# Two cached-attention layers, one core: the order of PE's and ACT's work at the change of layers

## The chip, the cores and the metric

The kernel runs on one core of a Trainium2 chip. The metric is the device time of one execution in microseconds, the median of several runs; lower is better. The profile is that of one further execution. Its engines are PE (matmuls; the loading of a stationary operand is shown apart, as PEld), DVE, ACT and POOL, and SP, which here only issues transfers. The kernel's name for the 128-partition on-chip memory that holds all large data is `mem`; `tps`, `sps` and `mps` are buffers in the accumulator memory that PE writes to (PSUM).

## The reference

Two layers are computed for a batch of 2 and one new token each (D = 576). Each layer is attention over a cache and then a mixer with an MLP, each behind a layer norm and added to x:

```python
# attention: H = 32 heads, Sk = 16384 cached positions, Dh = 128
q = (x @ wq).reshape(B, Sq, H, Dh).transpose(0, 2, 1, 3)
scores = jnp.einsum("bhqd,bhkd->bhqk", q, k_cache) * (Dh ** -0.5)
p = _softmax(scores, axis=-1)
o = jnp.einsum("bhqk,bhkd->bhqd", p, v_cache)
return o.transpose(0, 2, 1, 3).reshape(B, Sq, H * Dh) @ wo
# mixer and MLP: F = 4608
h = _gelu(_layernorm(x) @ w1)            # its columns are then shifted along S, which is 1
x1 = x + hs @ w2                         # hs: the shifted columns
return x1 + _gelu(_layernorm(x1) @ w3) @ w4

x = x + _A_ref(_layernorm(x), K, V, wq, wo)
x = x + _B_ref(_layernorm(x), w1, w2, w3, w4)     # and both once more, with the same weights and cache
```

With S = 1 the shifted columns are zero, so the mixer adds nothing; the kernel still multiplies zeros by w2. K and V are 268 MB each in bfloat16 and are read in both layers; the weights are some 20 MB per layer.

## The kernel before, in words

**Units.** There are 64 units (2 batches x 32 heads), numbered u. The K of a unit is a tile of 4 MB, 128 partitions x 128 blocks of 128 values, its V another. `mem` has six slots of one tile each and ahead of them a small region (AUX, `kt`) that holds three transposed chunks; a chunk is 8 blocks. In the main loop (`attention`, L994 to L1056, a hardware loop over three units a turn) half of the blocks of a K tile are transposed on PE (`transposed`, L1148, matmuls at L1158, into one of four buffers `tps`), copied to `kt` by ACT (`evacuate`, L1174) and multiplied by q on PE (`scores`, L1184); the other half are multiplied and summed by DVE (`dots`, L1215 and L1219), with q broadcast to all partitions (`q_broadcast`, L1112: DVE makes `diag`, L1115, PE multiplies, L1119, ACT copies, L1122). One unit behind follow the softmax (`softmax_max`: DVE, then POOL for the maximum over partitions, L1232; `softmax_exp`: ACT, L1240 to L1246) and the product with V (`pv`, L1272, four groups of 32 matmuls; a step of `keep_o` copies the result away).

**Order of the work.** Every engine executes its own list in order. `Graph` records each operation when the Python code calls it, so the order of calls is the order on each engine, and derives the semaphore waits from the named buffers that an operation reads and writes. An operation recorded with `to=` signals one engine alone; if another engine has to wait for it, it waits for the next operation of the same engine without `to=` (`_stand_in`). All transfers are issued by SP in the order of a plan (`plan_all`); `Store.pump` issues the next one as soon as its place in `mem` is free, in the order of the queue and never past one that has to wait.

**The change of layers.** Layer 1 takes the units in the order 63, 61, 62, 0, 1, ... and finds K of units 61 to 63 and V of 62 and 63 still in five of the slots. Slot 0 (with AUX) is all that is free for the weights: wo of layer 0, w3, w4, wq of layer 1, and then V of unit 61 in four parts. Each of these pieces lies where earlier ones lay, so it can be issued when PE has multiplied those. K of unit 0 then goes to the slot of K63, K of unit 1 in two halves to that of K61, V0, K2, V1 and so on to the next.

Between the loops run, in this order: `last_head` (the last scores, softmax and PV of layer 0, and wo: `shares` and `normed` divide by the sums, `dealt` lays the heads' outputs out for wo as `oA`, three quarters of the heads, and `oB`, the last quarter; `heads_projection`, matmuls at L893, multiplies wo's five pieces), `two_norms`, `cols_projection` with w3 (L823, L833; six pieces), `gelu_z`, `groups_projection` with w4 (L893 again; eight pieces; `side_norm` among them), `input_norm` of layer 1, and `q_projection` with wq (L823, L833; five pieces).

Through all of this K63 is prepared for the first unit of layer 1. `ahead` (L668) has PE transpose a chunk of K63 into `tps`; `lay` (L686, ACT at L692) copies it back over its own place. 14 of its 16 chunks are done so. When q of layer 1 is known, `early_scores` (L1200) multiplies these chunks straight from their place by q: first the chunks of which DVE does the scores in other units (b of 32 and more in both halves), then the rest; the last two chunks of the second half are transposed only then and go the usual way. DVE copies the part of the scores that it would have made itself to `s_dve` (L1033) and enters the loop.

Where the calls of `ahead` and `lay` stand in the kernel before: in `last_head` of layer 0 ahead(2) behind `normed`, ahead(2) and lay(2) behind `dealt`, lay(2) behind `touch(ACT.Sqrt)`, ahead(1) behind the first piece of wo, ahead(2) and lay(2) behind the second and the third, lay(4) behind the last; in `two_norms` ahead(2) and lay(4); in w3 ahead(3) and lay(2) ahead of the last piece; behind each w4 piece but the first ahead(1) and lay(1), in `input_norm` ahead(2) and behind each wq piece but the last ahead(1) and lay(1), by which time little or nothing is left for them.

The first two pieces of wo need `oA` alone. In the kernel before all four groups of PV run first, then piece 0, the layout of `oB`, and pieces 1 to 4.

## Time and profile before

| what | before |
|---|---|
| median of 3 runs | 2562.14 us (2562.13 to 2563.07) |
| profiled execution | 2561.02 us |
| its span, from first to last instruction | 2559.2 us |
| PE, PEld busy | 64%, 62% |
| DVE, ACT busy | 74%, 47% |
| DMA: queue of the transfers | 99.7% of 16 engines' span, 1094.23 MB |
| read from HBM, over the span | 428 GB/s |

A line of a timeline gives the start in us from the span's start, the length in us, engine, line of the kernel, operation, what is written and read, the number of instructions merged, and in brackets the idle time of the engine before it with what ended it; "issue" means that nothing the profile shows was waited for. A line of a table by stretches gives the stretch and its length, busy time (and number of instructions) of PE, PEld, DVE, ACT and POOL, the granted clock of PE as a share of full speed, the DMA share and GB/s. SPq rows are transfers at their issue. A row of the transfers' list ends with size in KB and the us from issue to landing.

### The profile page before, as it was taken

The page shows a single profiled execution, that of the slowest core. Times are in us where ns is not written, and L with a number is a line of the kernel's source. Part 1 is how long each engine was busy: PE and PEld are TensorE (multiplying, and loading weights), DVE is VectorE, ACT ScalarE, POOL GpSimd, SP SyncE. Part 2 cuts the span into 40 slices and gives each one's busy share as a digit, 9 for nine tenths or more (in the row PEclk, how much of TensorE's full clock was granted, in tenths as well). Part 3 has the DMA queues.
Part 4 walks back from the last instruction along what each step waited for, and adds up shares of the span by engine and source line. Part 5 has one row for each costly group of instructions (what it writes and reads, how often), then busy time and mean ns, then how long its engine had stood idle before and what let it go on. Part 6 is the DMA issues. An engine that isn't in the chain of part 4 may idle for free.

```text
span 2559.2 us, 75096 instructions
## 1 busy us (share of the span) xinstructions
PE 1629.4 (64%) x34456; PEld 1593.6 (62%) x34456; DVE 1889.5 (74%) x1925; ACT 1214.9 (47%) x1831; POOL 162.2 (6%) x151
## 2 busy tenths in 40 slices
PE   3766666666656666665777756666665666666566
PEld 3666566656656666665767756665665665666566
DVE  5877777777777777777549877777777777777774
ACT  2544444544444454444445544454444444445442
POOL 0000000000000000000000000000000000000000
PEclk8655555555555565556555655555555556555555
DMA  9999999999999999999999999999999999999999
GB/s 410 428 432 433 431 431 433 431 431 432 433 430 432 433 430 433 432 431 431 411 374 428 433 431 431 433 431 430 433 433 431 431 433 431 431 433 432 430 434 379
DMA packets 44762, 1094.82 MB, mean 428 GB/s; under 512 B 4907, under 2 KB 6319, under 8 KB 9391
## 3 DMA queue, kind: packets, MB, share of 16 engines
q1 hardware_dynamic: 44718, 1094.23, 99.7%
q8 instruction: 29, 0.48, 0.1%
q14 instruction: 15, 0.11, 0.0%
HBM read 1094.21 MB, written 0.00 MB: 428 GB/s over the span
## 4 chain that ended last, share of the span: by engine, by line
DMA 66%; DVE 19%; issue 8%; PE 6%; DVEq 0%; ACT 0%; SPq 0%; POOLq 0%; ACTq 0%
DMA mem<-in_A_k_cache_dram 64%; DVE prod L1215 9%; DVE s_dve L1219 8%; PE tps L1158 2%; DMA mem<-in_B_w_dram 2%; PE mps L1272 2%; PE sps L1119 1%; DMA mem<-in_A_wq_dram 0%; PE sps L1184 0%; PE sps L893 0%; DVE diag L1115 0%; DVE mx L1229 0%; PE sps L823 0%; DVE q_col L1109 0%; DVE o_acc L1253 0%
## 5 line engine op out<-in xcount | busy, mean ns | idle before, releaser
L1174 ACT ACTIVATE mem<-tps 128x1024 bf16<-128x1024 bf16 x1018 | 1029.4, 1023 | 848.9 <-PE tps L1158 827.0
L1219 DVE TENSOR_REDUCE s_dve<-prod 128x16 f32<-128x2048 bf16 x508 | 1161.2, 2286 | 17.4
L1158 PE MATMUL tps<-ident,mem 128*128 128x128 bf16 x8256 | 1010.9, 301 | 151.0 <-POOLq L187 147.7
L1215 DVE TENSOR_TENSOR prod<-mem,qb 128x2048 bf16<-128x2048 bf16 x508 | 621.4, 1223 | 537.0 <-POOLq L187 516.0
L1272 PE MATMUL mps<-p,mem 128*128 128x1 bf16 x16384 | 515.0, 166 | 608.1 <-ACT p L1246 608.1
L1272 PEld LDWEIGHTS mps<-p,mem 128*128 128x128 bf16 x16384 | 487.5, 104 | 618.8 <-ACT p L1246 618.8
L1158 PEld LDWEIGHTS tps<-ident,mem 128*128 128x128 bf16 x8256 | 770.8, 136 | 160.8 <-POOLq L187 157.0
L1184 PEld LDWEIGHTS sps<-q_col,mem 128*128 128x128 bf16 x8144 | 410.8, 114 | 4.7 <-ACT mem L1174 4.7
L1184 PE MATMUL sps<-q_col,mem 128*128 128x1 bf16 x8144 | 398.3, 170 | 4.1 <-ACT mem L1174 3.9
L1232 POOL PARTITION_ALL_REDUCE mx<-mx x128 | 160.2, 1252 | 2344.2 <-DVE mx L1229 2344.2
L1240 ACT ACTIVATE mx<-mx 128x1 f32<-128x1 f32 x128 | 25.9, 203 | 340.0 <-POOL mx L1232 339.9
L1119 PE MATMUL sps<-diag,ones_bf 128*128 128x128 bf16 x129 | 37.1, 287 | 114.3 <-DVE diag L1115 114.3
L1119 PEld LDWEIGHTS sps<-diag,ones_bf 128*128 128x128 bf16 x129 | 13.5, 105 | 124.8 <-DVE diag L1115 124.8
L1122 ACT ACTIVATE qb<-sps 128x128 bf16<-128x128 f32 x129 | 35.7, 277 | 65.9 <-PE sps L1119 65.9
L1242 ACT ACTIVATE p<-s_dve,mx 128x64 bf16<-128x64 f32 x128 | 44.5, 348 | 15.5
L1246 ACT ACTIVATE p<-sps,mx 128x64 bf16<-128x64 f32 x128 | 37.5, 293 | 0.0
L1227 DVE TENSOR_REDUCE mx<-sps 128x1 f32<-128x64 f32 x128 | 27.4, 214 | 7.3 <-PE sps L1184 7.3
L1115 DVE TENSOR_SCALAR diag<-ident,q_f 128x128 bf16<-128x128 bf16 x129 | 31.5, 244 | 0.0
L823 PE MATMUL sps<-xn,mem 128*128 128x2 bf16 x544 | 21.4, 174 | 9.4 <-DMA mem<-in_A_wq_dram 8.3
L823 PEld LDWEIGHTS sps<-xn,mem 128*128 128x128 bf16 x544 | 20.5, 122 | 10.1 <-DMA mem<-in_A_wq_dram 8.8
L1225 DVE TENSOR_REDUCE mx<-s_dve 128x1 f32<-128x64 f32 x128 | 26.7, 208 | 0.0
L1246 ACT ACTIVATION_READ_ACCUMULATOR p<-sps,mx (+1 forms) x128 | 24.2, 189 | 0.0
(112 smaller groups left out, 223.4 us busy)
## 6 DMA issues: line engine op xcount, KB each, us to landing
mem<-in_A_v_cache_dram SPq DMA_DIRECT2D x125, 4096.0 KB, 47.2
mem<-in_A_k_cache_dram SPq DMA_DIRECT2D x124, 4096.0 KB, 40.9
mem<-in_B_w_dram SPq DMA_DIRECT2D x10, 864.0 KB, 14.7
mem<-in_A_wq_dram SPq DMA_DIRECT2D x8, 1024.0 KB, 12.8
mem<-in_B_w_dram SPq DMA_DIRECT2D x7, 1152.0 KB, 15.7
mem<-in_A_wo_dram SPq DMA_DIRECT2D x6, 1152.0 KB, 35.8
mem<-in_A_v_cache_dram SPq DMA_DIRECT2D x4, 1024.0 KB, 8.8
mem<-in_A_k_cache_dram SPq DMA_DIRECT2D x2, 2048.0 KB, 13.1
```

Of the source, the lines that this page charges most:

```text
L823: ins = pe.matmul(out[:, m * B:(m + 1) * B], lhsT=buf[:, c:c + 127 * d + 1:d], rhs=self.xn[:, k, :], start=first and m == lo, stop=False, ...
L1119: self.pe(lambda pe: pe.matmul(qps, lhsT=self.ones_bf[:, :], rhs=self.diag[:, :], start=True, stop=True, skip_group_check=True), reads=["o ...
L1122: self.act(lambda e: e.activation(out=self.qb[s % self.NS][:, :], in_=qps, func=ACT.Copy), reads=[("qps", i)], writes=[("qb", s % self.NS) ...
L1158: ins = pe.transpose(self.tps[t][:, j * 128:(j + 1) * 128], buf[:, j * 128:(j + 1) * 128], self.ident[:, :])
L1174: self.act(lambda e: e.activation(out=self.kt[k], in_=self.tps[t][:, :].rearrange("p (i c) -> p i c", i=self.CH), func=ACT.Copy), reads=[( ...
L1184: ins = pe.matmul(self.sps[sp][:, c * self.CH + j:c * self.CH + j + 1], lhsT=self.kt[k][:, j, :], rhs=self.q_col[:, sp:sp + 1], start=True ...
L1215: self.dv(lambda e: e.tensor_tensor(out=prod, in0=buf.rearrange("p (j d) -> p j d", d=128), in1=qbc, op=ALU.mult), reads=[("qb", s % self. ...
L1219: self.dv(lambda e: e.tensor_reduce(out=sd[:, c0:c0 + DB], in_=prod, axis=AX.X, op=ALU.add), reads=["prod"], writes=[("s_dve", s % self.NS ...
L1232: self.pool(lambda e: e.partition_all_reduce(self.mx[:, 3, m:m + 1], self.mx[:, 2, m:m + 1], channels=128, reduce_op=ROP.max), reads=[("mx ...
L1242: self.act(lambda e: e.activation(out=p[:, n:self.NB], in_=self.s_dve[s % self.NS][:, :], func=ACT.Exp, bias=self.mx[:, 4, m:m + 1], scale ...
L1246: self.act(lambda e: e.activation(out=p[:, 0:n], in_=self.sps[i][:, 0:n], func=ACT.Exp, bias=self.mx[:, 4, m:m + 1], scale=self.scale, acc ...
L1272: ins = pe.matmul(self.mps[:, 448:449], lhsT=buf[:, j * 128:(j + 1) * 128], rhs=p[:, col:col + 1], start=(h == 0 and b == 0), stop=(h == 1 ...
```

## The change

Four things move; no operation of the reference's computation is added or left out.

- In `last_head`, piece 0 of wo is multiplied behind the first of the four groups of PV, and piece 1 behind the last, ahead of the layout of `oB`. All calls of `ahead` there go; one chunk is transposed at the end of `attention`, ahead of the last scores, and one `lay` stays, behind the softmax. The copy that makes `every` (the spread mask, L1068) stands ahead of `softmax_max`.
- The other chunks are transposed in `two_norms` (three), behind w3 (one), behind the first five pieces of w4 (one each), in `input_norm` (two, with their copies) and behind the first four pieces of wq (one each). The last two of these four are the two chunks that the kernel before transposed after q was known; they are kept in `tps` (`held_over`) until the loop's buffers are free.
- In `q_projection` of layer 1 the first unit's column of q is written straight to `q_col`, ahead of the copies to `q_f`.
- `early_scores` takes the chunks half by half, in the order of the blocks, and the broadcast for the next unit stands behind the second chunk instead of ahead of the first.

```diff
@@ __init__
+        self.held_over = []
@@ ahead
             if self.made == len(self.early):
-                return
+                if len(self.held_over) < self.LEAD:
+                    c = 2 * self.PB // self.CH - self.LEAD + len(self.held_over)
+                    self.transposes(1, 0, self.order(1)[0], c)
+                    self.held_over.append((0, self.order(1)[0], c, self.chunk))
+                    self.chunk += 1
+                continue
@@ input_norm
         self.touch(ACT.Exp)
+        self.lay(1 - l, 2)
@@ two_norms
-        self.ahead(l, 2)
+        self.ahead(l, 3)
@@ cols_projection
-            if w == "w3" and i == len(order) - 2:
-                self.ahead(l, 3)
-                self.lay(l, 2)
...
+        if w == "w3":
+            self.ahead(l, 1)
@@ q_projection
-        for s, u, n in self.runs(l):
+        if l:
+            at = self.order(l)[0]
+            self.dv(lambda e: e.tensor_copy(out=self.q_col[:, 0:1], in_=q[:, at:at + 1]),
+                    reads=[("sps", 2)], writes=[("q_col", 0)])
+        for s, u, n in self.runs(l)[l:]:
@@ groups_projection
-            if i >= 1:
+            if i < 5:
                 self.ahead(l, 1)
+            if i < 6:
                 self.lay(l, 1)
@@ attention
-            self.q_column(0)
-            self.q_broadcast(1)
-            for h, b, col in self.early:
+            pend += self.held_over
+            for h, b, col in sorted(self.early):
                 self.early_scores(l, o[0], h * self.BP + b, col)
-            for c in range(2 * n - LEAD, 2 * n):
-                self.transposes(l, 0, o[0], c)
-                pend.append((0, o[0], c, self.chunk))
-                self.chunk += 1
+                if (h, b) == (0, self.CH):
+                    self.q_broadcast(1)
...
         self.g.loop(first, (U - 1) // NS, NS)
+        self.ahead(l, 1)
         while pend:
@@ last_head
+        self.dv(... self.every ...)
         self.softmax_max(s)
         self.keep_o(s - 1)
-        self.dv(... self.every ...)
         self.shares(0, first)
         self.normed(l, 0, first)
-        self.ahead(l, 2)
         self.dealt(0, late, self.sps[2], ("sps", 2), self.masked[0], self.oA[:, :], "oA")
-        self.ahead(l, 2)
-        self.lay(l, 2)
         self.softmax_exp(s)
         self.touch(ACT.Sqrt)
-        self.lay(l, 2)
+        self.lay(l, 1)
         self.shares(first, U)
         self.landed("v", u, False)
-        for g in range(4):
+        self.pv(l, s, u, 0)
+        self.heads_projection(l, 0)
+        for g in range(1, 4):
             self.pv(l, s, u, g)
         self.keep_o(s, None)
         self.normed(l, first, U)
-        self.heads_projection(l, 0)
-        self.ahead(l, 1)
+        self.heads_projection(l, 1)
         self.dealt(late, U, self.sps[0], ("sps", 0), self.masked[1], self.oB[:, :], "oB")
-        for i in range(1, len(self.cuts["wo", l])):
+        for i in range(2, len(self.cuts["wo", l])):
             self.heads_projection(l, i)
-            if i < 3:
-                self.ahead(l, 2)
-                self.lay(l, 2)
-        self.lay(l, 4)
```

More of the change, by code (lines that the diff above doesn't have):

```diff
@@ L1065, in last_head @@
         every = bass.AP(tensor=i.tensor, offset=i.offset, ap=[list(i.ap[0]), [1, hg], [0, hg], [hg, 128 // hg]])
+        self.dv(lambda e: e.tensor_copy(out=self.every.rearrange("p (j h m) -> p j h m", j=hg, h=hg), in_=every),
+                reads=["ident"], writes=["prod", "every"])
         self.softmax_max(s)
         self.keep_o(s - 1)
[L1068 to L1069 removed]
         self.shares(0, first)
         self.normed(l, 0, first)
[L1072 removed]
         self.dealt(0, late, self.sps[2], ("sps", 2), self.masked[0], self.oA[:, :], "oA")
[L1074 to L1075 removed]
         self.softmax_exp(s)
         self.touch(ACT.Sqrt)
[L1078 removed]
+        self.lay(l, 1)
         self.shares(first, U)
         self.landed("v", u, False)
[L1081 removed]
+        self.pv(l, s, u, 0)
+        self.heads_projection(l, 0)
+        for g in range(1, 4):
             self.pv(l, s, u, g)
```

4 lines of the change are left out of this document (1 added, 3 removed).

## The prediction

> **What bounds the kernel now.** I read the page first: the span, the slices and the chain that ended last.
>
> ```profile
> span 2559.2 us, 75096 instructions
> DMA  9999999999999999999999999999999999999999
> DMA 66%; DVE 19%; issue 8%; PE 6%; DVEq 0%; ACT 0%; SPq 0%; POOLq 0%; ACTq 0%
> ```
>
> Every slice says 9 for DMA and two thirds of the chain is K arriving: the kernel is bound by its transfers, so an edit can gain only where they pause. The second view is busy time by stretches; its last two columns are DMA share and GB/s.
>
> ```profile
> 1270.00:1292.00 22.00, 19.10 (x413) 18.66 (x411) 4.65 (x29) 8.85 (x12) 0.00 (x0) 0.51 0.85 309
> 1292.00:1324.00 32.00, 19.34 (x498) 17.96 (x495) 7.52 (x31) 8.43 (x13) 0.00 (x0) 0.55 1.02 420
> 1324.00:1334.00 10.00, 6.58 (x115) 6.50 (x116) 9.79 (x11) 6.25 (x11) 1.25 (x1) 0.50 0.74 286
> 1334.00:1360.00 26.00, 22.19 (x471) 22.02 (x469) 22.87 (x21) 15.66 (x22) 1.25 (x1) 0.52 1.00 416
> 1360.00:1400.00 40.00, 29.27 (x633) 28.69 (x631) 37.64 (x39) 23.55 (x38) 3.76 (x3) 0.57 1.01 433
> ```
>
> The reader is to see two holes, both at the change of layers. Weights flow at 420 GB/s, so 309 over 22 us loses 22 x (1 - 309/420) = 5.8 us. Tiles flow at 433, so 286 over 10 us loses 3.4, and 416 over 26 us another 1.0. **The ceiling is 10.2 us**, and nothing outside this stage can give more: from 1360 us the rate is full. The end does not move either; there the last w4 pieces are awaited from DMA:
>
> ```profile
> 2553.58 1.60 PE L893 MATMUL mps<-prod,mem 128*128 128x2 bf16 x45 [1.17 <-DMA mem<-in_B_w_dram]
> ```
>
> The third view is SP's queue: when each load was issued, and what it waited for.
>
> ```profile
> 1271.89 0.33 SPq L98 DMA_DIRECT2D mem<-in_B_w_dram  x1
> 1281.01 9.17 SPq L98 DMA_DIRECT2D mem<-in_B_w_dram  x6
> 1326.81 0.33 SPq L98 DMA_DIRECT2D mem<-in_A_k_cache_dram  x1
> SPq L98 <- PE sps L893: 7.8, 1, 7.8
> SPq L98 <- PE sps L1184: 9.3, 1, 9.3
> ```
>
> Five of six slots hold kept K and V, so all weights pass through one slot: w3 is loaded into the place of wo as each wo piece is multiplied (L893), w4 into that of w3 (L823), wq into that of w4, V61 into that of wq, and K0 waits until the kept K63 is scored. The holes are these waits, so the sum follows PE. The orders of SP's and POOL's own instructions are the same in both kernels; only the moments at which their waits end move.
>
> **The change, step by step.** Below, a pair is one weight load with its matmul, and times are those of the profiled execution.
>
> ```profile
> 1262.83 1.17 POOL L1232 PARTITION_ALL_REDUCE mx<-mx  x1 [10.22 <-DVE mx L1229]
> 1264.10 1.94 ACT L692 ACTIVATE mem<-tps 128x1024 bf16<-128x1024 bf16 x2 [2.47 <-PE tps L1158]
> 1265.93 0.20 ACT L1240 ACTIVATE mx<-mx 128x1 f32<-128x1 f32 x1
> 1267.43 3.37 PE L1272 MATMUL mps<-p,mem 128*128 128x1 bf16 x128
> 1270.66 1.21 PE L893 MATMUL sps<-oA,mem 128*128 128x2 bf16 x40
> 1272.53 0.41 PE L940 MATMUL sps<-otn,prod 128*128 128x16 bf16 x8
> 1274.20 1.23 PE L893 MATMUL sps<-oA,mem 128*128 128x2 bf16 x40 [1.26 <-issue]
> 1279.72 1.25 PE L893 MATMUL sps<-oB,mem 128*128 128x2 bf16 x40
> 1285.00 4.83 PE L823 MATMUL sps<-xn,mem 128*128 128x2 bf16 x108
> ```
>
> *Step 1, to the first wo piece.* The maximum is ready at 1264.00 (POOL's row), but ACT evacuates two transposed chunks until 1266.04 before it serves the softmax. With them gone the softmax starts about 1.9 us sooner; but the chunk put ahead of the last scores costs PE 0.8 of it, so PV starts near 1266.5 instead of 1267.43. The copy of 1.06 us that spreads the mask (L1068) moves into time in which DVE waits for the scores, more than 3 us; without that cover it would delay the softmax by its length. oA is then made by about 1266.6, ahead of the first wo piece. A quarter of PV (0.85) and 40 pairs (1.2) end at 1268.6, so the first w3 load goes out 3.3 us sooner, the second (96 pairs of PV, 2.5, and 1.2) at 1272.4. By then w3's place is empty and wo's last pieces are still arriving, so the hole at 1272 closes.
>
> *Step 2, a stall that stays.* PE's row at 1274.20 waited 1.26 us for nothing that a semaphore shows. Layer 1 shows the like:
>
> ```profile
> q8 instruction: 1, 0.02, 1.7%
> 2521.33 3.55 PE L1272 MATMUL mps<-p,mem 128*128 128x1 bf16 x128
> 2528.79 1.23 PE L893 MATMUL sps<-oA,mem 128*128 128x2 bf16 x40 [1.56 <-issue]
> ```
>
> Counting pairs from the loop's end, both stalls come after exactly 248 (layer 0: 16+4+16+8+16+4+128+40+8+8; layer 1: 16+4+8+4+128+40+8+40), and in 1270 to 1274 us the instruction queue moved one packet. So I read it as the next block of code, asked for one block (124 pairs) earlier: pair 124 passes 60 and 92 pairs into the rows of 128, at 1269.0 and 2523.9, and PE goes on 5.2 and 4.9 us later. The change leaves the code up to the loop's end as it is, and reaches pair 124 at 1268.9. Hence PE stops again after the second wo piece (pair 248) and goes on at 1274.1. The price is bounded by 0 (a wait can't gain) and 1.7 us (1272.4 to 1274.1); I take 1.7, to which both rows are nearest. [...]
>
> Behind it stand 8 pairs of L940 (0.4) and two wo steps of 1.25 with no transposes between (before: 6.8 us from 1274.20 to 1280.97), so wo ends at 1277.0, **3.9 us sooner**.
>
> *Step 3, norm and w3.* From there to L823 were 4.03 us; three chunks of transposes instead of two reach about 0.1 past the norm, so L823 starts at 1281.2, **3.8 us sooner**. The last half of w3 and the w4 pieces are loaded as L823 frees their places (the six loads from 1281.01 on end 4 us behind its start), so w4 flows 3.8 us sooner. The hole there shrinks and does not go, since the queue runs dry before w3 is multiplied.
>
> ```profile
> 1291.53 2.72 PE L1158 MATMUL tps<-ident,mem 128*128 128x128 bf16 x24
> 1296.27 1.66 PE L893 MATMUL mps<-prod,mem 128*128 128x2 bf16 x60 [1.38 <-DVE prod L984]
> 1304.69 0.67 PE L893 MATMUL mps<-prod,mem 128*128 128x2 bf16 x15 [0.19 <-DMA mem<-in_B_w_dram]
> 1308.05 0.99 PE L823 MATMUL sps<-xn,mem 128*128 128x2 bf16 x32
> 1316.08 1.01 PE L823 MATMUL sps<-xn,mem 128*128 128x2 bf16 x32 [1.82 <-DMA mem<-in_A_wq_dram]
> ```
>
> *Step 4, w4 and wq.* The 2.72 us of transposes inside w3 go. Eleven chunks come back around the w4 and wq pieces, 0.9 us each (a third of that row). w3 takes 4.8 us and 60 more pairs (3.0), the gelu 1.4, so w4 starts at 1290.4. 180 pairs (5.8; 60 take 1.66 where none waits, 15 take 0.67), five chunks (4.5) and the statistics (0.6) bring PE to 1301.3; the landings, which PE awaited before, end w4 at 1305.4 - 3.8 = 1301.6. The norm takes 2.7 (1305.36 to 1308.05), and two chunks under it reach 0.6 past it: 1304.9. Four wq pieces (3.6) and four chunks (3.6) end at 1312.1; wq's last piece, awaited before until 1316.08, lands at 1312.3. So the cover just suffices, and wq ends at **1313.3, 3.8 us sooner**; where it is gone, each chunk costs its 0.9. A chunk also waits until ACT has copied the one four before it (1.0 each); behind such a wait stand the next weight piece on PE and, through its place, SP's next load. Four PSUM buffers hide that wait as long as PE takes more than ACT's 1.0 us from chunk to chunk, which all but the two under the norm do.
>
> ```profile
> 1317.90 0.24 DVE L1115 TENSOR_SCALAR diag<-ident,q_f 128x128 bf16<-128x128 bf16 x1
> 1318.29 3.17 PE L1200 MATMUL sps<-q_col,mem 128*128 128x1 bf16 x112
> 1320.99 1.23 DVE L1215 TENSOR_TENSOR prod<-mem,qb 128x2048 bf16<-128x2048 bf16 x1 [0.55 <-issue]
> 1325.55 1.04 PE L1158 MATMUL tps<-ident,mem 128*128 128x128 bf16 x8 [2.36 <-issue]
> 1337.98 1.23 DVE L1215 TENSOR_TENSOR prod<-mem,qb 128x2048 bf16<-128x2048 bf16 x1 [2.09 <-ACT qb L1122]
> 1353.57 1.22 DVE L1215 TENSOR_TENSOR prod<-mem,qb 128x2048 bf16<-128x2048 bf16 x1 [0.69 <-ACT qb L1122]
> 1355.15 0.33 SPq L98 DMA_DIRECT2D mem<-in_A_k_cache_dram  x1
> mem<-in_A_k_cache_dram SPq DMA_DIRECT2D x1, 4096.0 KB, 13.3
> mem<-in_A_k_cache_dram SPq DMA_DIRECT2D x1, 4096.0 KB, 15.7
> ```
>
> *Step 5, K63's scores.* The pairs now wait only for a short copy of q; 16 run before the broadcast, which comes 1.1 us behind wq as it did (1317.1 to 1318.2), and 96 (2.7 us) behind it, ending at 1313.3 + 3.85 = 1317.2. The last two chunks are already transposed, and K0's load no longer waits for a later score to signal them: it goes out at 1317.2, **9.6 us sooner**, before V61 has landed. The 3.4 us hole closes. But DVE's copy of the scores (in front of its first dots) now waits for all the pairs, so these dots start 0.8 behind them, at 1318.0, only 3.0 sooner.
>
> *Step 6, what is late next.* Now the loop's start-up binds. PE's stop of 2.36 us at the loop's head I read as the next code block, seven after pair 124: pair 992 passed at 1319.7 and passes at 1315.0, so PE starts 4.7 sooner. DVE waited 2.09 us at 1337.98 for the broadcast that PE made late; now DVE's own chain decides: 1318.0, 14.9 for a head's dots (1337.98 - 2.09 - 1320.99) and 0.7 for the broadcast as one head later, 1333.6, 4.4 sooner. K2's load hangs on that head: 1355.15 - 4.4 = 1350.8. It took 15.7 us to land, behind a queue (the last row), where K0, into an empty one, took 13.3 (the row above it). Now the queue has run dry when K2 is issued: 1350.8 + 13.3 = 1364.1 instead of 1370.8. After it DMA is the slower again: a head's 8.4 MB take 19.4 us at 433 GB/s, its dots 14.9. **The sum: 6.7 us**, out of 10.2; the rest is a new wait at K1's second half and K2.
>
> The profiled execution took 2561.02 us (its span and 1.8 around it), 1.1 below the median of the runs. On the median: 2562.14 - 6.7 = **2555.4**.
>
> **Rivals.** *The code block arrives in time.* PE goes on at 1272.4, everything up to K2 is 1.7 us sooner, sum 8.4: 2553.7. For it: the other blocks up to the loop stopped PE by nothing that shows; against it: the two rows of the stall. [...] *The transposes are only moved.* Step 4's cover is within 0.2 us; if each of the four wq chunks, or ACT's copies that free their buffers, adds 0.75, wq ends 3 us later, K2 too, and 3.7 remain: 2558.4, within 0.2%. For it: PE's idle time in 1292 to 1324 is 12.7 us, and eleven chunks take 9.5. *Slower: code blocks take longer once the holes are gone.* PE's code from pair 124 to the loop is seven blocks; 992 pairs were passed at 1319.7. At 5.2 us a block PE is not held. Blocks bind at all from about 6.6 us, and from 7.6 on the gain is gone (1268.9 + 7 x 7.6 = 1322.1; K2's load goes out 2.4 later than before and lands, drained, when it did). At 8.6 pair 992 passes at 1329.1, 9.4 later than before, and K2 lands 7.0 later: 2569. Against it: layer 1 measured 4.9 with DMA full.
>
> **How the numbers follow.** The forecast has 0.52, the timely block 0.13, the moved transposes 0.25, slow blocks 0.10. A difference of 0.2% (5.1 us) is about what a measurement of this kernel can tell from no change. The range reaches from just beyond the timely block, 2553.2, to 2559.6, which holds the moved transposes with an error of 1 us. Faster by over 0.2% means under 2557.0: all of the first rival and nine tenths of the forecast, 0.60; within 0.2%, 0.30; slower, 0.10.
>
> **What would show it.** First w3 load 3.3 us sooner; PE idle by "issue" after the second wo piece; L823 near 1281; a shorter hole near 1284; no hole before K0, a new one near K1 or K2. No pause at all up to 1360 us, or a wq that ends later than 1314, would make the prediction wrong.

## The result, and the profile after

| | before | after |
|---|---|---|
| median of 13 runs each, side by side | 2562.23 us (2561.03 to 2563.47) | 2556.41 us (2554.78 to 2557.78) |
| profiled execution | 2561.02 us | 2555.16 us |
| its span | 2559.2 us | 2553.4 us |

The ratio is 0.9976, with a 95% interval of 0.9967 to 0.9984: 5.8 us or 0.24% less. The forecast was 2555.4 us. The lines of the code have moved: L823 and L833 are now L830 and L840, L893 is L903, L940 is L950, L1158 is L1161, L1184 is L1187, L1200 is L1203, L1215 is L1218, L1115 and L1119 are L1118 and L1122.

The page of the changed kernel, span and chain that ended last:

```profile
span 2553.4 us, 75093 instructions
DMA 63%; DVE 21%; issue 9%; PE 5%; DVEq 0%; SPq 0%; ACT 0%; POOLq 0%; ACTq 0%
```

Transfers still carry the chain; DVE and "issue" have a little more of it. The same five stretches as in the prediction, of the changed kernel, with DMA share and GB/s last:

```profile
1270.00:1292.00 22.00, 17.78 (x422) 17.03 (x420) 5.46 (x34) 6.04 (x10) 0.00 (x0) 0.50 0.98 368
1292.00:1324.00 32.00, 24.86 (x535) 23.19 (x533) 8.95 (x27) 15.06 (x19) 0.00 (x0) 0.50 1.03 425
1324.00:1334.00 10.00, 7.68 (x160) 7.52 (x159) 9.28 (x11) 6.88 (x12) 1.25 (x1) 0.50 0.99 419
1334.00:1360.00 26.00, 19.61 (x414) 19.29 (x412) 24.79 (x24) 16.34 (x26) 2.51 (x2) 0.63 0.97 395
1360.00:1400.00 40.00, 32.49 (x710) 31.99 (x708) 37.34 (x35) 22.27 (x33) 2.50 (x2) 0.54 1.01 433
```

With the prediction's reckoning (420 GB/s for weights, 433 for tiles) the first hole lost 5.8 us and loses 22 x (1 - 368/420) = 2.7; the second lost 3.4 and loses 0.3; 1334 to 1360 lost 1.0 and loses 26 x (1 - 395/433) = 2.3; 1292 to 1324 runs 0.4 better than the reference rate. Together 4.9 us are lost instead of 10.2. The reader is to see two holes shrink and one grow.

What is won here arrives at the end undiminished. The last run of 45 w4 matmuls in layer 1, which began at 2553.58, begins 5.8 us sooner:

```profile
2547.80 1.61 PE L903 MATMUL mps<-prod,mem 128*128 128x2 bf16 x45 [1.18 <-DMA mem<-in_B_w_dram]
```

PE at the change of layers, timeline of the changed kernel:

```profile
1266.91 0.99 PE L1275 MATMUL mps<-p,mem 128*128 128x1 bf16 x32
1267.76 1.21 PE L903 MATMUL sps<-oA,mem 128*128 128x2 bf16 x40
1268.83 2.70 PE L1275 MATMUL mps<-p,mem 128*128 128x1 bf16 x96
1271.39 1.21 PE L903 MATMUL sps<-oA,mem 128*128 128x2 bf16 x40
1274.48 0.38 PE L950 MATMUL sps<-otn,prod 128*128 128x16 bf16 x8 [1.88 <-issue]
...
1281.00 4.81 PE L830 MATMUL sps<-xn,mem 128*128 128x2 bf16 x108
...
1290.97 0.94 PE L903 MATMUL mps<-prod,mem 128*128 128x2 bf16 x30 [1.51 <-DMA mem<-in_B_w_dram]
...
1312.95 1.01 PE L830 MATMUL sps<-xn,mem 128*128 128x2 bf16 x32 [0.56 <-DMA mem<-in_A_wq_dram]
...
1314.97 2.74 PE L1203 MATMUL sps<-q_col,mem 128*128 128x1 bf16 x96
1321.67 1.03 PE L1161 MATMUL tps<-ident,mem 128*128 128x128 bf16 x8 [3.96 <-issue]
...
1333.47 0.29 PE L1122 MATMUL sps<-diag,ones_bf 128*128 128x128 bf16 x1 [0.45 <-DVE diag L1118]
```

The wo pieces stand around PV, and PE stops after the second for 1.88 us with nothing to wait for that the profile shows, before the loop for 3.96. The last wq piece starts 3.1 us sooner than before (1316.08), the loop's first transposes 3.9 (1325.55). DVE in the same stretch, and SP's queue:

```profile
1317.75 0.23 DVE L1041 COPY s_dve<-sps 128x64 f32<-128x64 f32 x1 [2.92 <-PE sps L1203]
1318.52 1.22 DVE L1218 TENSOR_TENSOR prod<-mem,qb 128x2048 bf16<-128x2048 bf16 x1 [0.55 <-issue]
1334.11 1.22 DVE L1218 TENSOR_TENSOR prod<-mem,qb 128x2048 bf16<-128x2048 bf16 x1 [0.69 <-ACT qb L1125]
```

```profile
1269.00 23.76 SPq L98 DMA_DIRECT2D mem<-in_B_w_dram  x14
1317.74 18.28 SPq L98 DMA_DIRECT2D mem<-in_A_k_cache_dram  x3
1351.28 0.33 SPq L98 DMA_DIRECT2D mem<-in_A_k_cache_dram  x1
```

K0 is issued 9.1 us sooner, K2 3.9 sooner (from 1355.15 to 1351.28). The transfers' list of the changed kernel gives what K2 then took:

```profile
mem<-in_A_k_cache_dram SPq DMA_DIRECT2D x1, 4096.0 KB, 13.9
```

1351.28 + 13.9 = 1365.2 instead of 1355.15 + 15.7 = 1370.8: K2 lands 5.7 us sooner, and that is the whole gain.

### The profile page after: what moved, and what is told of

It is laid out like the page before. It is cut to its first block, busy times and chain, and to the rows that moved or that the text cites. A ratio compares the mean times of both kernels' runs of the same rounds, so it can differ in the third digit from the quotient of the medians.

```text
span 2553.4 us, 75093 instructions
## 1 busy us (share of the span) xinstructions
PE 1629.1 (64%) x34456; PEld 1592.5 (62%) x34456; DVE 1889.3 (74%) x1924; ACT 1215.6 (48%) x1831; POOL 160.5 (6%) x151
## 4 chain that ended last, share of the span: by engine, by line
DMA 63%; DVE 21%; issue 9%; PE 5%; DVEq 0%; SPq 0%; ACT 0%; POOLq 0%; ACTq 0%
DMA mem<-in_A_k_cache_dram 61%; DVE prod L1218 10%; DVE s_dve L1222 9%; DMA mem<-in_B_w_dram 2%; PE tps L1161 2%; PE mps L1275 2%; PE sps L1122 1%; DMA mem<-in_A_wq_dram 0%; PE sps L1187 0%; DVE diag L1118 0%; PE sps L903 0%; DVE mx L1232 0%; DVE q_col L1112 0%; DVE o_acc L1256 0%; DVE mx L1230 0%
## 5 line engine op out<-in xcount | busy, mean ns | idle before, releaser
L1161 PE MATMUL tps<-ident,mem 128*128 128x128 bf16 x8256 | 1011.0, 301 | 152.9 <-POOLq L187 148.1
L1218 DVE TENSOR_TENSOR prod<-mem,qb 128x2048 bf16<-128x2048 bf16 x508 | 621.3, 1223 | 534.0 <-POOLq L187 512.2
L1161 PEld LDWEIGHTS tps<-ident,mem 128*128 128x128 bf16 x8256 | 770.0, 136 | 162.5 <-POOLq L187 157.4
L1187 PEld LDWEIGHTS sps<-q_col,mem 128*128 128x128 bf16 x8144 | 410.5, 113 | 5.0 <-ACT mem L1177 4.8
L1187 PE MATMUL sps<-q_col,mem 128*128 128x1 bf16 x8144 | 398.2, 170 | 4.3 <-ACT mem L1177 4.1
L1122 PE MATMUL sps<-diag,ones_bf 128*128 128x128 bf16 x129 | 37.0, 287 | 114.0 <-DVE diag L1118 113.9
L1122 PEld LDWEIGHTS sps<-diag,ones_bf 128*128 128x128 bf16 x129 | 13.4, 104 | 124.6 <-DVE diag L1118 124.6
L1118 DVE TENSOR_SCALAR diag<-ident,q_f 128x128 bf16<-128x128 bf16 x129 | 31.6, 245 | 0.0
L830 PE MATMUL sps<-xn,mem 128*128 128x2 bf16 x544 | 21.5, 174 | 6.7 <-DMA mem<-in_A_wq_dram 4.8
L1256 DVE COPY o_acc<-mps 128x1 f32 (+1 forms) x130 | 19.2, 148 | 8.4 <-PE mps L1275 8.4
L830 PEld LDWEIGHTS sps<-xn,mem 128*128 128x128 bf16 x544 | 20.6, 122 | 7.8 <-DMA mem<-in_A_wq_dram 5.5
## 6 DMA issues: line engine op xcount, KB each, us to landing
mem<-in_A_wq_dram SPq DMA_DIRECT2D x8, 1024.0 KB, 12.6
mem<-in_A_k_cache_dram SPq DMA_DIRECT2D x2, 2048.0 KB, 10.2
```

The lines of the kernel that those rows point to most:

```text
L830: ins = pe.matmul(out[:, m * B:(m + 1) * B], lhsT=buf[:, c:c + 127 * d + 1:d], rhs=self.xn[:, k, :], start=first and m == lo, stop=False, ...
L1122: self.pe(lambda pe: pe.matmul(qps, lhsT=self.ones_bf[:, :], rhs=self.diag[:, :], start=True, stop=True, skip_group_check=True), reads=["o ...
L1161: ins = pe.transpose(self.tps[t][:, j * 128:(j + 1) * 128], buf[:, j * 128:(j + 1) * 128], self.ident[:, :])
L1187: ins = pe.matmul(self.sps[sp][:, c * self.CH + j:c * self.CH + j + 1], lhsT=self.kt[k][:, j, :], rhs=self.q_col[:, sp:sp + 1], start=True ...
L1218: self.dv(lambda e: e.tensor_tensor(out=prod, in0=buf.rearrange("p (j d) -> p j d", d=128), in1=qbc, op=ALU.mult), reads=[("qb", s % self. ...
```

## The experiments

Each run is told by three things: the stage times in its profile, the time at which K2 landed, and a **marker**, the distance from the load of K that SP issues near 1202 us, well inside layer 0, to that of the K of unit 11 in layer 1, near 1500. It takes the change of layers out of the rest of the span. These are its rows in the kernel before:

```profile
1202.51 0.33 SPq L98 DMA_DIRECT2D mem<-in_A_k_cache_dram  x1
1504.78 0.33 SPq L98 DMA_DIRECT2D mem<-in_A_k_cache_dram  x1
```

and in the changed kernel:

```profile
1202.47 0.33 SPq L98 DMA_DIRECT2D mem<-in_A_k_cache_dram  x1
1499.09 0.33 SPq L98 DMA_DIRECT2D mem<-in_A_k_cache_dram  x1
```

302.27 us before and 296.62 after, 5.65 less. All runs together; GB/s are those of the first four stretches, "loss" is the prediction's reckoning over all five:

| kernel | GB/s | loss | K2 issued + landing | marker | profiled | median (runs) | before beside it |
|---|---|---|---|---|---|---|---|
| before | 309, 420, 286, 416 | 10.2 | 1355.15 + 15.7 | 302.27 | 2561.02 | 2562.23 (13) | |
| after | 368, 425, 419, 395 | 4.9 | 1351.28 + 13.9 | 296.62 | 2555.16 | 2556.41 (13) | 2562.23 |
| after again (e9) | 375, 425, 411, 389 | 5.2 | 1351.40 + 14.3 | 297.49 | 2556.74 | 2556.74 (11) | 2561.85 |
| old scoring (e1) | 382, 375, 418, 422 | 6.5 | 1351.24 + 15.1 | 297.81 | 2557.20 | 2558.06 (11) | 2561.95 |
| scoring alone (e2) | 302, 417, 430, 391 | 9.3 | 1355.56 + 13.4 | 300.32 | 2561.06 | 2560.67 (11) | 2561.95 |
| PV first (e3) | 356, 428, 407, 391 | 5.9 | 1352.10 + 14.2 | 297.78 | 2556.11 | 2556.11 (10) | 2561.95 |
| DVE's share first (e4) | 379, 424, 411, 406 | 4.1 | 1350.72 + 13.4 | 296.17 | 2554.28 | 2555.35 (8) | 2561.95 |
| the same again (e11) | 377, 422, 419, 404 | 4.4 | 1350.79 + 14.5 | 296.79 | 2556.57 | 2556.01 (11) | 2562.15 |
| PV first, DVE's share first (e10) | 364, 420, 412, 387 | 6.3 | 1352.46 + 13.4 | 297.62 | 2555.87 | 2555.70 (11) | 2562.15 |
| 24 pairs (e5) | 382, 429, 403, 394 | 4.2 | 1350.86 + 12.9 | 295.92 | 2555.22 | one run | 2562.15 |
| 24 pairs, DVE's share first (e12) | 376, 430, 403, 408 | 3.8 | 1349.85 + 15.1 | 296.37 | 2554.41 | 2555.48 (11) | 2561.76 |
| 74 pairs at w4 (e6) | 368, 413, 409, 369 | 7.7 | 1353.90 + 14.7 | 300.17 | 2559.74 | 2557.72 (11) | 2561.85 |
| 74 pairs, DVE's share first (e7) | 360, 416, 407, 372 | 7.8 | 1354.26 + 12.6 | 299.16 | 2558.01 | 2557.57 (11) | 2561.85 |
| wq chunks twice (e8) | 375, 404, 398, 379 | 7.7 | 1353.57 + 14.3 | 299.65 | 2558.22 | 2556.69 (11) | 2561.85 |

**K2's landing is the gain, by the marker.** K2 lands sooner than 1370.8 by 5.7 us (after), 5.1 (e9), 4.5 (e1), 1.9 (e2), 2.2 (e6), 2.9 (e8); the marker is shorter by 5.65, 4.8, 4.5, 1.95, 2.1 and 2.6. In the other kernels the two agree within 0.8 us (most apart in e7, 3.9 and 3.1). So from there on little is won or lost. The medians do not follow as closely: e3, e10, e6 and e8 are better than their K2 landing says, by 1.3, 1.5, 1.9 and 2.3 us.

**How much a difference means.** The same kernel twice (e9) moved the stage times up to K2's issue by 0.1 to 0.5 us, the marker by 0.9 and the median by 0.3.

> The changed kernel once more, to learn how far marker and stages of one kernel differ from execution to execution. Expected: L830 at 1281.0, wq's end at 1314.0, K2 at 1351.3 within 0.3 each, marker 296.6 within 0.4.

The marker came out at 297.49, beyond what was expected, and L830 at 1280.53, 0.5 us sooner where 0.3 was expected. K2's issue (1351.40) agreed; its landing varies (13.9, 14.3). Markers that differ by less than 0.9 are not told apart.

### The scoring of K63, undone and alone (e1, e2)

e1 is the changed kernel with the old scoring, e2 the kernel before with the new scoring: the column of q written first, the last two chunks transposed ahead of time, chunks by halves. (In e2 these two come among the w4 pieces, at 1298.25 and 1300.25, not in `input_norm` as its expectation says.) The edit of e1, cut; e2 is the reverse in the other kernel:

```diff
@@ ahead
-                if len(self.held_over) < self.LEAD:
...
-                continue
+                return
@@ q_projection
-        if l:
-            at = self.order(l)[0]
-            self.dv(lambda e: e.tensor_copy(out=self.q_col[:, 0:1], in_=q[:, at:at + 1]),
-                    reads=[("sps", 2)], writes=[("q_col", 0)])
-        for s, u, n in self.runs(l)[l:]:
+        for s, u, n in self.runs(l):
@@ attention
-            pend += self.held_over
-            for h, b, col in sorted(self.early):
+            self.q_column(0)
+            self.q_broadcast(1)
+            for h, b, col in self.early:
...
+            for c in range(2 * n - LEAD, 2 * n):
+                self.transposes(l, 0, o[0], c)
```

> The changed kernel with K63 scored as before (last two chunks transposed only after q is known, broadcast first, q through q_f). Marker in all expectations: the time from the issue of K's load near 1202.5 us in layer 0 to that of K11 in layer 1, which is 302.27 us before and 296.62 us in the changed kernel, 5.65 less. Theory (PE's chain through wo, norm and w3 moves the weights 3.2 us sooner; the scoring order then moves K0 and DVE's chain decides K2): wq ends near 1314, K0's hole of about 3 us comes back, the loop starts 3.2 sooner than before and K2 is issued 3 sooner: marker 3.0 to 3.4 less than before, time 3.2 us under before. Rival (K0's hole costs nothing because the loop's start-up binds anyway): marker as in the changed kernel, 5.6 less.

> The kernel before with only the scoring part: two chunks held over from input_norm's calls, q straight to q_col, early scores half by half, broadcast after the second chunk. Theory: nothing moves up to wq's end (1317.1); K0 is issued about 5.5 us sooner than before (1321.3 instead of 1326.8), the hole ahead of it closes, but DVE's first dots start 0.5 to 1 later than before (1321.8 instead of 1321.0), K2 is issued 0.5 sooner and lands drained: marker 2.0 to 2.9 less than before, time 2.5 us under before. Rival (the gain is all in the tail of layer 0): marker within 0.5 of before. Rival (K0 sooner is worth its 5.5 us): marker 3.5 or more less.

In e1 the hole ahead of K0 is back, since K0 waits for the last scores: its stretch and K0's issue.

```profile
1292.00:1324.00 32.00, 24.04 (x523) 22.40 (x522) 10.39 (x28) 14.92 (x18) 0.00 (x0) 0.50 0.91 375
```

```profile
1323.21 12.18 SPq L98 DMA_DIRECT2D mem<-in_A_k_cache_dram  x3
```

The hole costs 3.4 us, yet the stretch behind it runs at 422 instead of 395, so e1 loses only 1.6 more than the changed kernel (6.5 against 4.9; marker +1.2). K2 was even issued at the same time (1351.24) but took 15.1 us to land, 1.2 more than there. In e2 the hole of 1324 to 1334 is gone (430 GB/s), and 1334 to 1360 falls from 416 to 391: the loop's first matmul came at 1325.96 as before (1325.55), and its dots started 1.8 us later, 1.1 of it because wq ended later (1318.19 instead of 1317.09), which was not expected. So e2 may understate the scoring. Of the scoring's 3.4 us hole, 1.2 to 2 reach the marker. The two halves by themselves save 3.9 and 1.3 us by the medians, 5.2 together; both at once 5.8. By these numbers what was moved out of the tail is two thirds to four fifths of the gain, and the scoring a fifth to a third. The scoring's share is not firm: e2's ratio of 0.9993 has an interval of 0.9984 to 1.0002, which holds no gain at all, and e1's marker is only 0.3 longer than e9's. e1 saved more by the marker (4.5) than was expected (3.0 to 3.4), e2 a little less than the lower end (1.95 against 2.0).

### PV ahead of wo, and the stop (e3, e5)

e3 puts all of PV ahead of wo's first piece again:

```diff
-        self.pv(l, s, u, 0)
-        self.heads_projection(l, 0)
-        for g in range(1, 4):
+        for g in range(4):
             self.pv(l, s, u, g)
         self.keep_o(s, None)
         self.normed(l, first, U)
-        self.heads_projection(l, 1)
+        self.heads_projection(l, 0)
...
-        for i in range(2, len(self.cuts["wo", l])):
+        for i in range(1, len(self.cuts["wo", l])):
```

> The changed kernel with PV and wo in the order of before (all four groups, then piece 0, layout of oB, pieces 1 to 4), transposes where the change has them. Theory (PE stops after pair 248 for its next code block whatever stands there): the stop ends near 1274.4 again, wo ends at 1277, L823's successor starts at 1281.0 as in the changed kernel; w3's first load goes out 2.5 us later and a hole of 1 to 1.5 us at 1272 comes back, but w3's last half hangs on PE, so w4 flows as soon: marker within 0.4 of the changed kernel, time the same as the changed kernel. Rival (what the change's first words say: the wo pieces around the last PV make the gain): marker 1 to 3 us more than in the changed kernel.

PE of e3, and then of e5, whose edit adds 24 pairs (a weight load of `ident` and a matmul of one column each) behind the first `shares`, where PE waits for the softmax:

```profile
1270.34 1.21 PE L903 MATMUL sps<-oA,mem 128*128 128x2 bf16 x40
1271.40 0.36 PE L950 MATMUL sps<-otn,prod 128*128 128x16 bf16 x8
1271.62 0.99 PE L903 MATMUL sps<-oA,mem 128*128 128x2 bf16 x32
1274.58 1.44 PE L903 MATMUL sps<-oA,mem 128*128 128x2 bf16 x48 [1.98 <-issue]
```

```diff
+    def pad(self, n):
...
+            for _ in range(n):
+                ins = pe.matmul(self.sps[1][:, 500:501], lhsT=self.ident[:, :], rhs=zero, start=True, stop=True,
...
@@ last_head
+        if l == 0:
+            self.pad(24)
```

> The changed kernel with 24 idle pairs (weight load and one-column matmul) on PE behind the first shares, ahead of PV, where PE waits for the softmax anyway. Code-block theory: the stop follows the count, so it comes after 16 of the 40 pairs of wo's piece 1 (224 of the old pairs) instead of behind them; the block is asked for 24 pairs (0.65 us) sooner, so PE goes on at 1273.4 to 1274.1 instead of 1274.48, and with 24 pairs (0.7 us) then still to do the norm's end and L830's first matmul (now some lines lower) stay within 0.3 us of 1281.0. Rival, the stop belongs to the instructions behind piece 1 (a wait that the profile does not show, of L950 for oB's source): the row of 40 stays whole and L950 has the stop as before.

```profile
1271.26 0.56 PE L903 MATMUL sps<-oA,mem 128*128 128x2 bf16 x16
1273.49 0.80 PE L903 MATMUL sps<-oA,mem 128*128 128x2 bf16 x24 [1.66 <-issue]
1274.15 0.36 PE L961 MATMUL sps<-otn,prod 128*128 128x16 bf16 x8
```

This is the cleanest reading of the study. In e3 the stop cuts a run of 40 equal matmuls after 32: 128 + 40 + 8 + 32 pairs, behind 40 that the changed kernel too has there after the loop, 248 in all. With 24 pairs ahead it falls 24 pairs sooner, after 16 of 40, as expected. That is no wait of one instruction for a result: it goes by the place in the code. (That a block of code arrives there is inferred, from the count and from the instruction queue. It moves a packet of 0.02 MB ahead of each such stop: at 1271.8 in the kernel before and 1272.0 in the changed one, in layer 1 at 2526.4 and 2520.3; PE goes on 2.4 to 2.5 us later, at 1274.20, 1274.48, 2528.79 and 2522.78. The trace does not say what a packet holds, or what asks for it and when.) PE goes on 1.0 us sooner (0.5 against e9's 1273.99), and L830 follows at 1280.65, a little outside the expected 0.3.

In e3 PE goes on at 1274.58 too, so wo ends within 0.2 us of the changed kernel's, and the first w3 load (1271.57 instead of 1269.00) costs 12 GB/s in the first stretch, 0.6 us. Its median is not above the changed kernel's (2556.11). Its marker is longer by 1.2, beyond the 0.4 that was expected and inside the rival's 1 to 3, but e9's is longer by 0.9. The stage times are sharper. K0's issue in e3, and in e10, which has the order of e3 too:

```profile
1318.56 18.28 SPq L98 DMA_DIRECT2D mem<-in_A_k_cache_dram  x3
1318.64 17.96 SPq L98 DMA_DIRECT2D mem<-in_A_k_cache_dram  x3
```

Without that order K0 is issued at 1317.74 (changed kernel), 1317.85 (e9), 1317.70 (e4) and 1317.77 (e11). **So the wo pieces around PV bring 0.7 to 0.9 us up to K0's issue, in two kernels; what of that reaches the time isn't resolved here.**

### Scored by halves or DVE's share first (e4, e11, e10)

```diff
-            for h, b, col in sorted(self.early):
+            for i, (h, b, col) in enumerate(self.early):
                 self.early_scores(l, o[0], h * self.BP + b, col)
-                if (h, b) == (0, self.CH):
+                if i == 1:
                     self.q_broadcast(1)
```

> The changed kernel with the early scores in the order of before (the chunks that DVE would score first, then the rest), the broadcast still after the second chunk scored. Theory (DVE's copy of these scores stands in front of its dots, and DVE's chain decides K2): DVE's first dots start 1.3 us sooner (1317.2 instead of 1318.5), K0's issue stays at 1317.7; PE, which starts the loop at 1321.7 behind its code block, then decides, so K2 is issued 0.4 to 0.6 sooner: marker 0.4 to 0.6 less than in the changed kernel. Rival (scoring by halves frees K63 sooner and so helps): marker more than in the changed kernel.

> The changed kernel with DVE's share of K63 scored first, once more, beside the run above and the same runs of the kernel before. If scoring by halves costs what the first such run read (0.45 us by the marker, about 1 us by the medians), the time is 2555.0 to 2556.0 and the ratio 0.9970 to 0.9978, marker 295.8 to 296.8, dots at 1317.0 to 1317.5. If the first run was only at the good end of the spread: 2556.2 to 2557.0, marker up to 297.8, the dots 1.3 us sooner than in the changed kernel all the same.

> The changed kernel with two of its four moves undone: PV whole ahead of wo's piece 0 (as in the kernel before), and K63's chunks scored with DVE's share first. If those two moves bring nothing, as the runs that undid each alone read, the time is that of the changed kernel or up to 1 us less: 2555.0 to 2556.6, ratio 0.9970 to 0.9980, DVE's first dots at 1317.0 to 1317.6, marker (K's load near 1202 us to the load of K11) 296.0 to 297.8. If the order around PV is worth its 1.2 us when the dots no longer hold K2, marker above 297.8 and time above 2556.8.

DVE of e4, its first dots:

```profile
1317.20 1.23 DVE L1218 TENSOR_TENSOR prod<-mem,qb 128x2048 bf16<-128x2048 bf16 x1 [0.55 <-issue]
```

1.3 us ahead of the changed kernel's (1318.52), while K0 is issued as it was (1317.70): K0 goes to the place of both halves and so waits for all of the scores either way. Scoring by halves therefore gives K0 nothing and holds DVE. Both runs met what was expected of the dots (1317.20, 1317.27); e4's marker is 0.45 shorter, as expected, e11's is 0.2 longer than the changed kernel's, and e11's median (2556.01) stands at the edge of the range for a real gain. They lie 6.6 and 6.1 us below the kernel before, against 5.8 and 5.1 of the changed kernel; the intervals of the ratios (0.9964 to 0.9985 and 0.9967 to 0.9985) overlap with the changed kernel's, so a gain of up to 1 us by the other order is possible, not shown. e10, with PV first as well, came out at 2555.70, also within the spread; its dots were 1318.14, later than the 1317.6 expected, and its marker 297.62. Its K2 was issued at 1352.46, 1.7 us later than e4's, since there PE decides: the loop's head came late, and DVE waited for the broadcast that PE made behind it.

```profile
1323.07 1.04 PE L1159 MATMUL tps<-ident,mem 128*128 128x128 bf16 x8 [4.46 <-issue]
1335.29 1.22 DVE L1216 TENSOR_TENSOR prod<-mem,qb 128x2048 bf16<-128x2048 bf16 x1 [2.21 <-ACT qb L1123]
```

### Idle pairs at the w4 pieces (e6, e7)

These were to pull the code of the loop's head forward: 54 and 20 idle pairs ahead of the first two w4 pieces, in PE's waits for DMA. e7 has DVE's share first as well.

```diff
@@ groups_projection
+            if l == 0 and i < 2:
+                self.pad((54, 20)[i])
```

> The changed kernel with 54 and 20 idle pairs (a weight load and a one-column matmul into an unused column) on PE ahead of the first and second w4 piece of layer 0, where PE waited 1.51 and 0.66 us for DMA; nothing else differs. Theory (PE's stop at the loop's head is the next code block, asked for when the block before it is entered, 992 pairs behind the first loop): 74 pairs more move that point back from the early scores to ahead of wq's last piece, so PE starts the loop 2.5 to 3.5 us sooner, near 1318.5 instead of 1321.7; but DVE's chain (dots from 1318.5) decides K2, so the marker stays within 0.3 of the changed kernel's 296.62. Rival (the stop belongs to the loop's entry itself): PE starts at 1321.7 again or later.

> The idle pairs of the kernel above together with the early scores in the order of before (DVE's chunks first). Theory: now both chains start sooner, DVE's dots at 1317.2 and PE near 1318.5; DVE's decides, K2 is issued 1.2 to 1.5 us sooner than in the changed kernel, marker 295.1 to 295.5: the two edits together gain three times what the better one gains alone (0.45), since each alone leaves the other chain in place. Rival (each edit gains by itself or not at all): marker no less than 296.0.

Both expectations failed. PE of e6:

```profile
1298.97 0.16 PE L903 MATMUL mps<-prod,mem 128*128 128x2 bf16 x1 [0.85 <-issue]
...
1316.03 2.72 PE L1216 MATMUL sps<-q_col,mem 128*128 128x1 bf16 x95
1320.14 0.19 PE L1216 MATMUL sps<-q_col,mem 128*128 128x1 bf16 x1 [1.39 <-issue]
1324.38 1.04 PE L1174 MATMUL tps<-ident,mem 128*128 128x128 bf16 x8 [4.05 <-issue]
```

A new stop holds the very last of the 96 early scores, which K0 waits for (1320.36, 2.6 us later) and in e6 DVE's dots too (1321.13); the loop's head waits 4.05 us as before. In e7 K0 is issued at 1320.38, the loop's head comes at 1324.66, and the marker is 299.16 (295.1 to 295.5 were expected). By the number alone e6's rival, a start at 1321.7 or later, came true.

The trace says more. The first row is one more stop, ahead of the last pair of the fourth w4 piece. From the stop behind wo's second piece (1274.45 in e6) PE runs 510 pairs up to it, and from there to the stop at the scores 384; e7's stops stand at the same two pairs. Read as four blocks and three, that is 128 pairs to a block (510/4 = 127.5, 384/3 = 128), not the 124 of the prediction. The boundary before the stop at the scores lies 128 pairs back (95 + 1 for the broadcast + 16, and 16 of the last wq piece, which began at 1314.01), so at about 1314.5, and PE goes on 5.6 us later. In the changed kernel, without the 74 pairs, the last boundary before the loop then lies behind 95 + 74 - 128 = 41 of the 96: 1314.97 + 41 x 0.0285 = 1316.1, and the loop starts 5.5 us later, at 1321.67. In e5 (24 pairs more) it is behind 17 of them, 1315.0, and the loop starts 5.6 us later, at 1320.63. So few pairs help and many harm, and one reading would cover both: a block is there 4.2 to 6.4 us after PE has entered the one before it. The ends of that range are e6's loop head (1320.14 to 1324.38) and its stop at w4.

For the loop's head this reading is argued, not shown: no count tells that a block begins there, though a packet of the instruction queue starts some 2.6 us ahead of PE there too (at 1319.0 in the changed kernel, 1322.9 in the kernel before). A rival does nearly as well: in all twelve kernels without the 24 pairs the loop's head came 3.6 to 4.5 us after the last early score, whatever the boundary. Only e5 and e12, at 3.3 and 3.1 us, speak for the place in the code.

The last run put the 24 pairs and DVE's share first together (the two edits above):

> Both edits that read a little ahead of the changed kernel, together: the 24 idle pairs behind the first shares and DVE's share of K63 scored first. If the pairs shift the block boundaries for good, as the look at them alone read, the stop comes after 16 pairs of wo's piece 1 again, the loop's first matmul at 1320.3 to 1321.0 (before these pairs 1321.3 to 1322.0), DVE's first dots at 1316.2 to 1317.0, K2's load at 1349.8 to 1350.7, and the median is 2554.6 to 2555.8, ratio 0.9966 to 0.9975. If one look misled, the loop's first matmul is at 1321.3 or later and the time is that of DVE's share first alone, 2555.3 to 2556.3.

PE and DVE of e12:

```profile
1273.54 0.80 PE L903 MATMUL sps<-oA,mem 128*128 128x2 bf16 x24 [1.66 <-issue]
1320.64 1.03 PE L1174 MATMUL tps<-ident,mem 128*128 128x128 bf16 x8 [3.10 <-issue]
```

```profile
1317.07 1.23 DVE L1231 TENSOR_TENSOR prod<-mem,qb 128x2048 bf16<-128x2048 bf16 x1 [0.55 <-issue]
```

Stop, loop head and K2's issue (1349.85) came as expected, the dots 0.1 later, the median at 2555.48, ratio 0.9975 (0.9966 to 0.9984), 6.3 us below the kernel before. But K2, issued 1.4 us sooner than in the changed kernel, took 15.1 us and landed at 1364.95, hardly sooner than there (1365.2). Whether the loads ahead of it now hold it is open: e5's K2, issued at 1350.86, landed at 1363.8, and e11's, issued at 1350.79, at 1365.3.

### The cover under wq (e8)

The four chunks among the wq pieces are transposed twice:

```diff
@@ __init__
+        self.times = 1
@@ cols_projection
             if w == "wq" and i < len(order) - 1:
+                self.times = 2
                 self.ahead(1 - l, 1)
+                self.times = 1
                 self.lay(1 - l, 1)
@@ transposes
+        times = self.times
...
-            for j in range(self.CH):
+            for j in list(range(self.CH)) * times:
```

> The changed kernel with the four chunks under the wq pieces transposed twice each (32 more pairs of 0.1 us, the same result). Theory (PE's idle time under wq is only 0.95 us, so the cover of step 4 is used up): wq ends 2.2 to 2.5 us later, near 1316.4, DVE's dots and K2 as much later: marker 2.0 to 2.6 more than 296.62. Rival (PE's work under wq is hidden by transfers whatever it is): marker within 0.3.

DVE of e8, the first instruction behind wq:

```profile
1316.44 0.16 DVE L861 CAST q_col<-sps 128x1 bf16<-128x1 f32 x1 [10.43 <-PE sps L831]
```

2.4 us later than in the changed kernel (1314.00), as expected, for 3.4 us more of PE (a chunk takes 1.66 us instead of 0.81, four times). So the cover held 1.0 us more, its waits for DMA (0.39 and 0.56 us in the changed kernel), and was then used up. K2 landed 2.7 us later and the marker grew by 3.0 (2.0 to 2.6 were expected). The median, however, is 2556.69, 0.3 above the changed kernel's and no more than e9's; the profiled execution, 2558.22, was the second longest of its eleven (2555.54 to 2559.92). Why the others do not show the 3 us stays open, since only one execution of each kernel was profiled. The same holds in part for e6, whose profiled execution took 2559.74 at a median of 2557.72.

## Why the prediction was right, step by step

- **The ceiling and the holes.** Right. Losses went from 10.2 to 4.9 us, the new one lies at K1's second half and K2, and nothing behind 1360 us changed.
- **Step 1.** PV at 1266.91 (forecast 1266.5), first w3 load 2.9 us sooner (3.3), the second at 1272.63 (1272.4). The times were right, but e3 shows that the new order around PV, to which the step gave 3.3 us at the first load, hardly matters for wo's end: the stop behind it levels it out. 0.7 to 0.9 us of it are left at K0's issue (e3, e10).
- **Step 2, the stop.** Right, and the part that was least certain. It stayed at pair 248 in the changed kernel and in e3, and moved with 24 added pairs. It cost 1.88 us (1.7). The 124 pairs of a block were taken as half of 248; e6's stops read as 128, which moves pair 124 by about 0.1 us. The rival of a timely block is out, with stops of 1.88, 1.98 and 1.66 us in the changed kernel, e3 and e5.
- **Step 3.** L830 at 1281.00 (1281.2), 4.0 us sooner. The sentence that "w4 flows 3.8 us sooner" is **the first mis-sized term**: the first w4 piece landed 3.25 sooner, and wq ended 3.1 sooner instead of 3.8 (1313.96 against 1313.3). Its load from the transfers' list, first of the changed kernel, then of the kernel before:

```profile
mem<-in_B_w_dram SPq DMA_DIRECT2D x1, 864.0 KB, 6.6
```

```profile
mem<-in_B_w_dram SPq DMA_DIRECT2D x1, 864.0 KB, 5.8
```

  The issue came 4 us sooner, but the load took 0.8 longer; the last piece of w3 was under way beside it for 3.3 us, before the change for 1.9. This does not account for wq: in e9 the first w4 piece landed 3.8 us sooner, as forecast, and wq still ended at 1314.07. Where its 0.7 us are lost, between the first w4 piece and wq's last, stays open.
- **Step 4.** Right: the cover just suffices (PE still waits 0.56 us for the last wq piece) and is used up (e8). The rival "only moved" needed wq 3 us later than forecast; it was 0.7. (That rival's eleven chunks at 0.9 us are 9.9, not 9.5; the sum does not use it.)
- **Step 5.** K0 at 1317.74 (1317.2), dots at 1318.52 (1318.0): both late by 0.5, where wq was late by 0.7. The hole ahead of K0 closed. That DVE's copy would wait for all the scores was foreseen; e4 shows that it need not.
- **Step 6.** Right in its chain: DVE decides over PE (L1122 waits for `diag`), dots at 1334.11 (1333.6), K2 at 1351.28 (1350.8). **The second mis-sized term** is K2's landing, 13.9 instead of 13.3 us, and its reason was wrong: the queue had not run dry. V0's load, issued at 1337.76, took 17.1 us and was under way until 1354.9, 3.6 us behind K2's issue. The two terms, 0.5 and 0.6, make 6.7 into 5.7. The loop's head came 3.9 us sooner, not 4.7, since the last boundary ahead of it is passed at 1316.1 by e6's count, not at 1315.0; that cost nothing, because DVE decided. The slow-block rival is out by the same 3.9.

## What to carry to other kernels

Where transfers bound a kernel and pause only between stages, follow the one load whose landing restarts the full stream: here K2's issue plus its landing gave every kernel's marker within 0.8 us (the medians of e3, e6, e8 and e10 within 2.3), while the hole that was closed first (3.4 us ahead of K0) gave a third to a little over half of its size, because the next wait took over. Count straight-line PE code in matmul pairs: a stop by "issue" that stays at the same pair when the instructions there change (here pair 248, 1.88 us in the changed kernel and 1.98 in e3) was read here as code that arrives late, and work that came to it sooner won nothing: the kernel before came to it at 1272.94 and went on at 1274.20, the changed one at 1272.60 and 1274.48. Idle pairs shifted that point for good (24, two kernels) and for ill (74, two kernels), so look at where each boundary falls before adding or removing any.

## What was not expected of the hardware

- By the counts above the next block of code could be used 4.2 to 6.4 us after PE entered the one before it, and 128 dense pairs take some 3.6 us (16 pairs of scores take 0.6, 96 take 2.7), so by this reading code as dense as that has to stop. The longest stop, at the loop's head, grew from 2.36 to 3.96 us as the work ahead of it was removed. Whether the instruction queue's packets wait behind the bulk loads was not tried.
- A DMA share near 1 did not mean full flow. The changed kernel's transfers in 1282 to 1292 us:

```profile
DMA packets 668, 3.40 MB, mean 340 GB/s; under 512 B 78, under 2 KB 78, under 8 KB 665
q1 hardware_dynamic: 666, 3.37, 95.0%
```

  and the same hole of the kernel before, 1284 to 1296 us:

```profile
DMA packets 699, 3.63 MB, mean 302 GB/s; under 512 B 81, under 2 KB 81, under 8 KB 698
q1 hardware_dynamic: 698, 3.61, 81.7%
```

  At 95% of the time busy, the engines moved 340 GB/s, where 1292 to 1324 us had 425 at 101.5%. A packet was under way 0.23 us in the hole and 0.24 there, but it carried 5.1 KB instead of 6.2. Size alone is not the reason: 1296 to 1300 us moved 412 GB/s with packets of 3.3 KB. The cause is open. The last two columns of a stretch have to be read together, and a hole is better measured in GB/s.
